# A decode-attention kernel: three value loads paired in the load order, output projection on two column groups, last selection over two PSUM banks

## The chip, the cores and the metric

One NeuronCore of a Trainium2 (trn2) chip. The metric is the device time of one execution in microseconds (us), the median of several executions on the slowest (here: only) core. The span of a profile is some 1.8 us shorter than the time. Ratios are computed from runs of the same rounds on the same chip: the mean time of one kernel's fast runs over the mean of the other's, so they are not quite the ratio of the medians quoted beside them.

## The reference

One decoding step for 32 sequences with 32 query heads and 8 key/value heads of 128, over the last 512 positions of the cache:

```python
B, Sq, D = x.shape                      # 32, 1, 512
Hq, Dh = 32, 128
W = min(4096, max(256, Sk // 4))        # 512
q = (x @ wq)                            # -> 32 heads of 128
k = repeat(k_cache[:, :, Sk - W:, :], 4, axis=1)
v = repeat(v_cache[:, :, Sk - W:, :], 4, axis=1)
p = softmax(einsum("bhqd,bhkd->bhqk", q, k) * Dh ** -0.5)
o = einsum("bhqk,bhkd->bhqd", p, v)
return o.reshape(B, Sq, Hq * Dh) @ wo   # bf16 throughout
```

Keys and values of the window are 33.6 MB each, wq and wo 4.2 MB each: 75.5 MB must be read for very little arithmetic.

## The kernel before

Sixteen key loads K0..K15 and sixteen value loads V0..V15 of 2 MB go through one DMA queue (the sync engine's) in a fixed order, into three key buffers and four value buffers. VectorE transposes each key load (T), TensorE makes scores (S), VectorE and ScalarE the softmax (M, E, R, N), TensorE turns P (P, then C), both engines spread it into a block form (Z), and TensorE multiplies it with the values (V). The orders are written out by hand for every engine.

```python
DMA_ORDER = ("K0 K1 K2 V0 K3 K4 V1 K5 K6 K7 V2 K8 K9 V3 K10 V4 K11 K12 V5 K13 K14 V6 K15 V7 V8 V9 V10 V11 V12 "
             "V13 V14 V15").split()
DVE_ORDER = ("T0.0 T0.1 T1.0 T1.1 T2.0 T2.1 M0 R0 T3.0 Z0.0 ...").split()   # cut; the query comes ahead of it
...
nc.sync.dma_start(w_sb[:, 0:2, :]..., wq_rows[:, 0:wq_half])      # first half of wq
@block.sync
def _(sp):
    sp.dma_start(w_sb[:, 2:4, :]..., wq_rows[:, wq_half:])        # second half
    for name in DMA_ORDER:
        n = int(name[1:])
        if name[0] == "K":
            if n >= NK: sp.wait_ge(dve_T, 2 * (n - NK + 1))       # NK = 3: transposed, buffer free
            sp.dma_start(K_sb[:, n % NK]..., cache_rows(k_cache, n)).then_inc(sem_k[n % NK], 16)
        else:
            if n >= NV: sp.wait_ge(pe_PV, n - NV + 1)             # NV = 4: multiplied, buffer free
            sp.dma_start(V_sb[:, n % NV]..., cache_rows(v_cache, n)).then_inc(sem_v[n % NV], 16)
    ...                                                           # then wo in nine pieces
```

The end, on TensorE, VectorE and ScalarE (the last two share the copies):

```python
select(SELCUT, B, lambda i: S_ps[:, 0, i * NHG * nl:(i + 1) * NHG * nl])   # the last 8 sequences, one bank
for hg in range(NHG):                                  # 8 pieces of wo
    pe.wait_ge(sem_wo[hg], 16)
    for i in range(4):
        if hg == NHG - 1 and i == WO_CUT: pe.wait_ge(sem_last, 16)
        for c in range(4):                             # four column groups of 32
            ins = pe.matmul(X_ps[32*c:32*(c+1), 2, 0:128], lhsT=o_sel[:, i, hg, :],
                            rhs=wo_sb[:, hg, i, c*128:(c+1)*128], ..., tile_position=(0, 32*c))
...
for c in range(2):                                     # VectorE; ScalarE takes c = 2, 3
    dve.tensor_copy(out_sb[:, c, :], X_ps[32*c:32*(c+1), 2, 0:128])
```

## Time and profile before

| | before |
|---|---|
| time, median of the first 3 runs | 187.69 us (187.65 to 187.70) |
| profiled span | 185.9 us |
| bytes moved by the load queue | 75.53 MB |
| last piece of wo: first, median, last of 16 DMA engines done | 179.78, 181.30, 182.99 us |
| store of the result issued | 183.98 us |

A load runs on 16 DMA engines; the trace records when each of them reports its share complete. "First, median, last engine" below are these completion events of one load, in us from the span's start. The page's rows, the waits and the tail are shown and read in the prediction.

### The profile page before, as it was taken

How to read it: one execution, taken by the hardware profiler on the slowest of the kernel's cores; microseconds unless marked ns; L12 is line 12 of the kernel's file. 1: busy time of each engine (PE TensorE's matmuls, PEld its weight loads, DVE VectorE, ACT ScalarE, POOL GpSimd, SP SyncE). 2: the span in 40 equal slices, each digit the busy share in tenths (PEclk: the TensorE clock that was granted, in tenths of full speed). 3: DMA queues.
4: the chain of work that ended last, by engine and by line, in shares of the span. 5: the costliest groups of instructions: out<-in, count | busy, mean ns of one | idle time of the engine just before them, and what ended most of it. 6: DMA issues, size and time to landing. Idle time of an engine off the chain costs nothing.

```text
span 185.9 us, 3842 instructions
## 1 busy us (share of the span) xinstructions
PE 109.0 (59%) x1604; PEld 89.4 (48%) x1604; DVE 131.9 (71%) x239; ACT 82.3 (44%) x142; POOL 32.0 (17%) x82
## 2 busy tenths in 40 slices
PE   0232004336179906929906994159979975998752
PEld 0100001022069805819606974019949975987741
DVE  0006999689999999993699987999999995010001
ACT  3001000269320397020695018925998999910011
POOL 7100390500700080060240041000040000000000
PEclk9999999955557985885985599576999999999998
DMA  6999999999999999999999999999999999999980
GB/s 194 434 448 412 437 423 423 448 412 437 420 416 441 416 427 434 416 437 427 423 421 423 441 423 420 434 423 430 428 412 434 427 423 430 420 423 411 405 332 27
DMA packets 6304, 75.80 MB, mean 408 GB/s; under 512 B 720, under 2 KB 912, under 8 KB 1936
## 3 DMA queue, kind: packets, MB, share of 16 engines
q1 hardware_dynamic: 6240, 75.53, 96.4%
q8 instruction: 12, 0.20, 0.4%
q10 hardware_dynamic: 48, 0.03, 0.1%
q14 instruction: 4, 0.03, 0.0%
HBM read 75.53 MB, written 0.03 MB: 406 GB/s over the span
## 4 chain that ended last, share of the span: by engine, by line
DMA 64%; DVE 20%; PE 9%; issue 3%; SPq 3%; DVEq 0%
DMA V_sb<-in_v_cache_dram 31%; DMA K_sb<-in_k_cache_dram 14%; DMA w_sb<-in_wo_dram 12%; DVE KT_sb L431 12%; PE O_ps L356 8%; DMA w_sb<-in_wq_dram 6%; DVE w_sb L453 4%; DVE QA_sb L421 2%; SPq L214 2%; PE X_ps L299 1%; SPq L202 1%; DVE oT_sb L414 0%; DVE KT_sb L409 0%; PE X_ps L393 0%; DVE maxv L438 0%
## 5 line engine op out<-in xcount | busy, mean ns | idle before, releaser
L431 DVE STREAM_TRANSPOSE KT_sb<-K_sb 128x2048 uint32<-128x2048 uint32 x32 | 72.3, 2287 | 1.3 <-DMA K_sb<-in_k_cache_dram 1.1
L356 PE MATMUL O_ps<-w_sb,V_sb 128*128 128x128 bf16 x640 | 47.0, 244 | 9.6 <-DVE w_sb L453 5.0
L356 PEld LDWEIGHTS O_ps<-w_sb,V_sb 128*128 128x128 bf16 x640 | 45.6, 110 | 12.3 <-DVE w_sb L453 6.5
L268 POOL COPY QBD<-QA_sb 32x64 bf16<-32x64 bf16 x64 | 25.6, 540 | 81.2 <-PE S_ps L319 63.6
L520 ACT ACTIVATE w_sb<-PTc,mask 128x512 bf16<-128x512 bf16 x60 | 38.9, 729 | 0.0
L319 PE MATMUL S_ps<-KT_sb,QBD 128*32 128x512 bf16 x256 | 20.7, 475 | 26.6 <-DVE KT_sb L431 20.2
L453 DVE TENSOR_SCALAR w_sb<-PTc,mask 128x512 bf16<-128x512 bf16 x100 | 30.2, 370 | 6.3 <-PE O_ps L356 6.3
L319 PEld LDWEIGHTS S_ps<-KT_sb,QBD 128*32 128x32 bf16 x256 | 7.5, 110 | 36.5 <-issue 32.4
L492 ACT ACTIVATE X_ps<-S_ps,negmax 128x512 f32<-128x512 f32 x8 | 5.3, 657 | 42.8 <-DVE negmax L440 42.8
L338 PE MATMUL PT_ps<-P_bf,pick 128*128 128x128 bf16 x128 | 11.4, 260 | 17.9 <-ACT P_bf L501 14.7
L338 PEld LDWEIGHTS PT_ps<-P_bf,pick 128*128 128x128 bf16 x128 | 9.8, 119 | 20.9 <-ACT P_bf L501 16.3
L530 ACT ACTIVATE oT_sb<-O_ps 128x128 bf16<-128x128 f32 x8 | 6.0, 750 | 28.2 <-PE O_ps L356 28.2
L356 PE MATMUL O_ps<-K_sb,V_sb 128*128 128x128 bf16 x256 | 14.9, 217 | 3.5 <-DMA V_sb<-in_v_cache_dram 2.2
L356 PEld LDWEIGHTS O_ps<-K_sb,V_sb 128*128 128x128 bf16 x256 | 14.5, 96 | 4.3 <-issue 2.5
L520 ACT ACTIVATE K_sb<-PTc,mask 128x512 bf16<-128x512 bf16 x24 | 15.3, 725 | 1.6 <-DVE KT_sb L431 1.6
L453 DVE TENSOR_SCALAR K_sb<-PTc,mask 128x512 bf16<-128x512 bf16 x40 | 12.1, 377 | 0.3 <-ACT PTc L511 0.2
L474 DVE CAST K_sb<-S_ps 128x256 bf16<-128x256 f32 x1 | 0.4, 425 | 14.3 <-PE S_ps L368 14.3
L356 PE MATMUL O_ps<-KT_sb,V_sb 128*128 128x128 bf16 x128 | 7.5, 217 | 2.3 <-DMA V_sb<-in_v_cache_dram 2.3
L356 PEld LDWEIGHTS O_ps<-KT_sb,V_sb 128*128 128x128 bf16 x128 | 7.3, 96 | 2.5 <-issue 2.5
L520 ACT ACTIVATE KT_sb<-PTc,mask 128x512 bf16<-128x512 bf16 x12 | 7.7, 728 | 0.0
L501 ACT ACTIVATE P_bf<-X_ps,recip 128x512 bf16<-128x512 f32 x8 | 5.5, 684 | 4.5 <-DVE recip L446 4.4
L409 DVE CAST KT_sb<-X_ps 128x512 bf16<-128x512 f32 x1 | 0.7, 692 | 9.2 <-PE X_ps L299 9.2
(41 smaller groups left out, 49.6 us busy)
## 6 DMA issues: line engine op xcount, KB each, us to landing
K_sb<-in_k_cache_dram SPq DMA_DIRECT2D x16, 2048.0 KB, 15.1
V_sb<-in_v_cache_dram SPq DMA_DIRECT2D x16, 2048.0 KB, 16.8
w_sb<-in_wq_dram SPq DMA_DIRECT2D x2, 2048.0 KB, 9.7
w_sb<-in_wo_dram SPq DMA_DIRECT2D x7, 512.0 KB, 19.8
w_sb<-in_wo_dram SPq DMA_DIRECT2D x1, 384.0 KB, 22.6
w_sb<-in_wo_dram SPq DMA_DIRECT2D x1, 128.0 KB, 14.4
oT_sb<-in_x_dram ACTq DMA_DIRECT2D x1, 32.0 KB, 4.4
out_dram<-oT_sb SPq DMA_DIRECT2D x1, 32.0 KB, 1.5
```

What stands on the lines that cost most here:

```text
L214: sp.dma_start(wo_sb[:, hg, i0:i1].rearrange("p i n -> p (i n)"), wo[hg * 512:(hg + 1) * 512, :].rearrange("(m i) n -> m (i n)", i=4)[:, i ...
L268: pool.tensor_copy(dst[:, i, :, x0:x0 + 4], src).then_inc(pool_qbd, 1)
L319: ins = pe.matmul(S_ps[32 * c:32 * c + 32, q % 2, :], lhsT=QBD[:, q % 2, g, b, e, :], rhs=bass.AP(tensor=KT_sb, offset=s0 * slot + (b * G ...
L338: ins = pe.matmul(PT_ps[:, r, :], lhsT=pick[:, r, KS - s:KS - s + P], rhs=P_bf[:, s, :], start=(s == 0), stop=(s == KS - 1), tile_position ...
L356: ins = pe.matmul(O_ps[:, q % 2, 0:P], lhsT=V_sb[:, m % NV, r, :], rhs=z_of(q)[:, :, x0 + r, :], start=(e == 0 and r == 0), stop=(e == 1 a ...
L421: dve.tensor_copy(QA[32 * a:32 * a + 32, c], QW[32 * c:32 * c + 32, :, :, a::4].rearrange("p h k q -> p h q k"),).then_inc(dve_q, 1)
L431: dve.transpose(KT_w[:, n % NK, b].rearrange("p i r s -> p r i s"), K_w[:, n % NK, :, 32 * b:32 * b + 32],).then_inc(dve_T, 1)
L453: ins = dve.tensor_scalar(z_of(q)[:, k].rearrange("p x r -> p (x r)"), PTc[:, q % RING].rearrange("p x r -> p (x r)"), mask[:, k:k + 1], N ...
L492: act.activation(P_f32, S_ps[:, q % 2, :], ACTF.Exp, bias=negmax[:, q:q + 1], scale=SCALE, accum_out=sums[:, q:q + 1],).then_inc(act_exp, 1)
L501: act.activation(P_bf[:, :, :], P_f32.rearrange("p (x s) -> p s x", s=KS), ACTF.Copy, scale=recip[:, q:q + 1],).then_inc(act_P, 1)
L520: ins = act.activation(z_of(q)[:, k].rearrange("p x r -> p (x r)"), PTc[:, q % RING].rearrange("p x r -> p (x r)"), ACTF.Copy, scale=mask[ ...
L530: act.activation(oT_sb[:, :, 4 * q:4 * q + 4].rearrange("p h a -> p a h"), O_ps[:, q % 2, 0:P].rearrange("p (a h) -> p a h", a=4), ACTF.Co ...
```

## The change

Its intent: fewer, larger value loads (V0+V1, V4+V5, V6+V7 are each one DMA of 4 MB into two neighbouring buffers); K0 ahead of the second half of wq, so that VectorE can transpose while it would otherwise wait for the query; engine orders matched to it; at the end the last O tile and half of the last selection moved so that VectorE and ScalarE work side by side on two banks; and two matmuls of 256 columns for four of 128, so that one copy per engine remains.

```diff
-        "K0 K1 K2 V0 K3 K4 V1 K5 K6 K7 V2 K8 K9 V3 K10 V4 K11 K12 V5 K13 K14 V6 K15 V7 V8 V9 V10 V11 V12 "
-        "V13 V14 V15"
+        "K0 B0 K1 K2 K3 V0 K4 K5 K6 V2 K7 K8 V3 K9 K10 K11 V4 K12 K13 K14 V6 K15 V8 V9 V10 V11 V12 V13 V14 "
+        "V15"
 ... PE_ORDER, DVE_ORDER ("T0.0 T0.1 Q0 T1.0 ...") and ACT_ORDER likewise ...
+    V_PAIRED = (0, 4, 6)
-                    if n >= NV:
-                        sp.wait_ge(pe_PV, n - NV + 1)
+                    k = 2 if n in V_PAIRED else 1
+                    if n + k > NV:
+                        sp.wait_ge(pe_PV, n - NV + k)
                     sp.dma_start(
-                        V_sb[:, n % NV]..., cache_rows(v_cache, n)
+                        V_sb[:, n % NV:n % NV + k]..., cache_rows(v_cache, n, k)
 ...
-            select(SELCUT, B, lambda i: S_ps[:, 0, i * NHG * nl:(i + 1) * NHG * nl])
+            select(SELCUT, B, lambda i: S_ps[:, i // 2, (i % 2) * NHG * nl:(i % 2 + 1) * NHG * nl])
-                    for c in range(4):
+                    for c in range(2):
-                            X_ps[32 * c:32 * (c + 1), 2, 0:128],
+                            X_ps[32 * c:32 * (c + 1), 2, 0:256],
 ...
-            for c in range(2):
-                dve.tensor_copy(out_sb[:, c, :], X_ps[32 * c:32 * (c + 1), 2, 0:128])
+            dve.tensor_copy(out_sb[:, 0, :], X_ps[0:32, 2, 0:256])
 ... ScalarE: one copy of 256 columns; half of the last selection copy; the last O copy goes to VectorE ...
```

## The prediction

> **What bounds the kernel now.** I read the overview page first, then the sync engine's waits, then the last 10 us of the timeline, then a table by stage.
>
> ```profile
> PE 109.0 (59%) x1604; PEld 89.4 (48%) x1604; DVE 131.9 (71%) x239; ACT 82.3 (44%) x142; POOL 32.0 (17%) x82
> ...
> DMA  6999999999999999999999999999999999999980
> GB/s 194 434 448 412 437 423 423 448 412 437 420 416 441 416 427 434 416 437 427 423 421 423 441 423 420 434 423 430 428 412 434 427 423 430 420 423 411 405 332 27
> ...
> q1 hardware_dynamic: 6240, 75.53, 96.4%
> q8 instruction: 12, 0.20, 0.4%
> ```
>
> No compute engine is over 71%, but the row DMA has a 9 in every slice from the second to the 38th, and the rate stays between 405 and 448 GB/s there. The loads are one unbroken stream of 75.5 MB.
>
> ```profile
> K_sb<-in_k_cache_dram SPq DMA_DIRECT2D x16, 2048.0 KB, 15.1
> V_sb<-in_v_cache_dram SPq DMA_DIRECT2D x16, 2048.0 KB, 16.8
> ```
> ```profile
> SPq L202 <- DVE KT_sb L431: 94.6, 13, 21.6
> SPq L208 <- PE O_ps L356: 40.7, 7, 17.9
> SPq L219 <- ACT oT_sb L547: 13.4, 1, 13.4
> ```
>
> The queue waits 94.6 us for transposes and 40.7 us for value products before it may issue. That looks like the bound, and the chain of waits counts 20% for VectorE accordingly. It isn't: from issue to landing a load takes 15 to 17 us (median, first fence), although 2 MB move in 4.9 us, so each is issued with about two others still ahead of it. The shortest issue to landing in the trace is 10.7 us (a key load), still 5.8 us of queued work. The loads' completion events land every 4.89 us (median engine: 13.04, 17.94, 22.84, 27.73, ...), without a gap at any wait.
>
> ```profile
> core 0: us, PE busy (x) PEld busy (x) DVE busy (x) ACT busy (x) POOL busy (x), PEclk, DMA share, GB/s
> ...
> 111.00:156.00 45.00, 33.71 (x528) 29.55 (x525) 42.85 (x113) 37.59 (x66) 3.28 (x6) 0.89 1.00 425
> 156.00:171.00 15.00, 11.61 (x196) 11.48 (x197) 0.69 (x2) 7.85 (x14) 0.00 (x0) 1.00 1.00 421
> 171.00:179.40 8.40, 5.93 (x144) 5.49 (x144) 0.42 (x1) 0.72 (x1) 0.00 (x0) 1.00 1.02 405
> 179.40:183.00 3.60, 1.73 (x91) 1.09 (x77) 0.00 (x0) 0.00 (x0) 0.00 (x0) 1.00 0.38 146
> ```
>
> Even at 111 to 156 us, where VectorE is busy 42.85 of 45 us, the DMA share is 1.00. After 179.4 us the share falls to 0.38: most DMA engines have finished and a few run late. The completion events show it: all 16 engines land a load within 0.38 us of each other up to 47 us, within 1.8 us after that, within 3.3 us at the end. Each step follows one of the twelve 16 KB packets of the instruction queue: such a packet (about 1.05 us, and the next data packet lasts 1.1 instead of 0.61) makes one engine about 1.6 us late for good. Three engines are hit twice, and they set the last landing at 183.0 us; the mean engine is done about 1.8 us earlier.
>
> ```profile
> 178.24 0.42 DVE L474 CAST K_sb<-S_ps 128x256 bf16<-128x256 f32 x1 [14.28 <-PE S_ps L368]
> 178.72 1.30 PE L393 MATMUL X_ps<-w_sb,K_sb 128*32 128x128 bf16 x80 [0.52 <-DVE K_sb L474]
> ...
> 182.71 0.56 PE L393 MATMUL X_ps<-w_sb,K_sb 128*32 128x128 bf16 x16 [0.55 <-DMA w_sb<-in_wo_dram]
> 183.32 0.56 ACT L547 ACTIVATE oT_sb<-X_ps 32x128 bf16<-32x128 f32 x2 [5.81 <-PE X_ps L393]
> 183.32 0.59 DVE L477 CAST oT_sb<-X_ps 32x128 bf16<-32x128 f32 x2 [4.66 <-PE X_ps L393]
> 183.98 0.36 SPq L220 DMA_DIRECT2D out_dram<-oT_sb  x1
> ```
>
> The selection (its second copy ends at 178.66) and the output projection have caught up with the stream by 180.0 and then wait for each piece of wo. On the path after the last landing lie only the last four matmuls (to 183.3), the copies (to 183.91) and the store (to 185.9).
>
> **What the Trainium skill says.** (1) "DMA: Bandwidth & Descriptors", Where 436 GB/s comes from: 16 ports of 256 bits at 850 MHz give 435.2 GB/s. The trace agrees: the second to 36th slices average 427. (2) The same page, Measured, advises transfers of at least 1 MiB, and its anatomy section fits about 2.0 us fixed per DMA, on the software path. Merging two loads would pay that only where loads run one by one; landings 4.89 us apart for 8 packets of 0.614 us per engine leave no such gap here. (3) "Runtime: NRT & Kernel Launch", Instruction fetch mechanics: refills come in 16 KiB blocks of 256 instructions, TensorE holds 128 KiB, and crossing a block is "mostly hidden". The trace agrees on the blocks (twelve packets of 16 KB for some 3250 TensorE records); hidden from TensorE they are, but not from a saturated DMA engine. (4) "PSUM — Partial Sum Buffer", PSUM bank collisions: two engines may not touch the same bank and partition quadrant at once. So letting VectorE and ScalarE share the second selection copy needs two banks; no run here shows a collision.
>
> **The change part by part.**
>
> *Three value pairs (0+1, 4+5, 6+7).* Bytes are the same. Three DMAs fewer means three fewer completion packets per engine, at 9 ns each: 0.03 us. A pair has 32 KB per partition contiguous on both sides, so its packets may become 32 KB. The trace's packets took 46 ns (1 KB), 160 (4 KB) and 614 (16 KB): 37.8 ns per KB plus 8.7. If the packets double, each engine saves 8 x 8.7 ns = 70 ns a pair, 0.21 us for three. Estimate: 0.03 to 0.24 us, on the path. A fetch's 1.6 us stays.
>
> *K0 ahead of the second half of wq.* K0 lands at 13.2 instead of 18.1, the half at 18.1 instead of 13.2. VectorE transposes K0 (2 x 2.23 us) at 13.2 to 17.7, when it was idle. The query then starts when the half has landed: 18.1 + 1.9 for its matmuls = 20.1, + 6.3 us for copy, transpose and 16 copies = 26.4 (before: 15.2 to 21.5). T1 ends at 30.9, T2 at 35.4; before, T2 ended at about 34.8. Nothing is won or lost downstream.
>
> *Does the stream stay fed?* A load must be issued before the load ahead of it lands. With landings at 8.3 + 4.9 per load, walking the new order with durations of the old trace: K4 needs T1 (30.9), its slot opens at 42.5. K6 needs T3, which follows the first scores (3.6 us at the low clock), the maximum and R0: about 41; slot 53. K7 needs T4, behind Z0 and M1: about 53.4; slot 63.7. K10 needs T7, behind the first two value products (4.6 us each, to 60.4), M2 and Z1: about 75.4; slot 83.2. K11 needs T8: 79.9; slot 88. V4+V5 needs two products (60.4); slot 93. K14 needs T11: about 105.6; slot 112.6. V6+V7 needs four products (86.4); slot 117.5. V10 needs product 6, whose data now lands with its partner at 127.3: about 131; slot 142. The least slack is about 7 us. No starvation, so the reordered VectorE, ScalarE and TensorE work is worth 0.
>
> *Selection and last evacuation.* VectorE copies the last O tile (about 0.3 to 0.7 us, where ScalarE took 0.72), and the two engines each copy half of the selection (128x128 instead of 128x256 in 0.42 us). The projection may start some 0.3 us earlier than 178.7. It then waits for wo until 183.0 anyway: 0 on the path.
>
> *Output projection.* 64 matmuls of 256 columns instead of 128 of 128. The last 16 took 0.41 us to the end of the last when nothing held them back, so (0.41 - 0.22)/15 = 13 ns apart with four column groups. Two groups of twice the width should come 53 ns apart (estimate: half the array), about 107 ns per block of wo against 51: 3.4 us in all instead of 1.7. There is room: the 28 blocks before the last wo piece need 3.0 us from 178.5. After the last landing, one matmul of 256 takes about 0.27 us (193 ns at 64 columns, 219 at 128, 245 at 192) and the second follows 53 ns later, so TensorE ends 0.04 to 0.08 us later than before. Then VectorE makes one copy of 256 columns, about 0.425 us (its 128x256 copy above) against 0.59 for two: -0.165. ScalarE's single copy is about 0.38 (0.27 at 128 columns, 0.49 at 384), so VectorE's ends last. Net: about -0.1 us.
>
> *Fewer TensorE instructions.* 128 fewer load and matmul records, all at the end, is half a block. The twelfth fetch (180.9 us) may come later or fall away; it hits an engine that is not among the three latest. The double hits come from the ninth to eleventh fetches, 151.8 to 172.0, which stay: 0.
>
> Sum: -0.1 for the tail and -0.03 to -0.24 for the pairs: -0.13 to -0.34. 187.69 - 0.25 = 187.4 us.
>
> **The rivals.** *A starved queue*: the pair takes two slots at once and delays K15 behind V6+V7. For: TensorE runs at half clock in places (PEclk 5 in mid-kernel), and my walk is coarse. Against: 7 us of slack. It would cost 1 to 5 us and show as slices under 400 GB/s. *Other fetch luck*: if the double hits vanish the end comes up to 1.6 us earlier (186.0); if one engine is hit three times before the end, 1.6 us later (189). For: the fetches follow TensorE's progress, which the new order shifts. Against: the ninth to eleventh fall well before the last loads in either order. *The tail as the bound*: the two-group projection falls behind the wo stream; by its 3.4 us against the time from 178.5 to 183.0 it has about 1 us to spare. Failing, it costs 0.2 to 0.5 us. *The compute chain is the bound*, as the chain's 20% for VectorE suggests, and the reorder wins 2 to 4 us (184 to 185.5). Against: DMA share 1.00 throughout; fewer bytes or a better rate alone could do that, and the port limit leaves 2%.
>
> **Range and chances.** The three runs of before agree within 0.05 us. The pairs and the tail span 0.2 us; fetch luck and a small stall make up the rest: 186.7 to 188.0. Faster by over 2% means below 183.9, under what this stream allows without losing all engine skew: 3%. Slower by over 2% needs a long starvation: 2%.
>
> **What would show it.** Right: the DMA row still full from the second slice, 75.5 MB, landings 4.89 us apart, last wo landing within 0.4 us of 183.0, one final copy per engine of about 0.43 and 0.38 us, final matmuls waiting for wo. Wrong: slices under 400 GB/s before 170 us, engine spread at the end far from 3.3 us, a projection that doesn't wait for wo, or a last landing moved by more than a microsecond.

## The result, and the profile after

The changed kernel takes 187.24 us (187.13 to 187.36, 6 runs) against 187.67 us (187.29 to 187.85, 6 runs): ratio 0.9981, 95% interval 0.9968 to 0.9994. So it is faster by 0.3 to 0.5 us, about a fifth of a per cent: clear of noise.

The overview page after: busy times, the DMA rows in 40 slices, the two queues, the chain of waits.

```profile
PE 109.5 (59%) x1540; PEld 90.3 (49%) x1540; DVE 132.1 (71%) x239; ACT 81.2 (44%) x141; POOL 31.8 (17%) x82
...
DMA  6999999989999999999999999989999999999980
GB/s 201 428 445 424 431 421 484 445 367 424 424 421 445 413 435 421 428 435 410 458 438 392 445 410 442 463 382 442 415 431 431 410 438 417 438 410 416 400 338 30
...
q1 hardware_dynamic: 5808, 75.53, 96.5%
q8 instruction: 12, 0.20, 0.4%
...
DMA 41%; PE 22%; DVE 20%; ACT 7%; issue 6%; SPq 3%
```

Bytes and busy times are as before, 64 matmuls are gone, and the load queue carries 432 packets fewer: 384 for the pairs (768 packets of 16 KB have become 384 of 32 KB in the records) and 48 completion packets. The slices with an 8, or with 367, 392 and 382 GB/s, look like holes but aren't: one or two slices ahead of each stand 484, 458 and 463, more than any slice of before. The low slices lie at the ends of the three pairs (which land at 42, 101 and 125 us), and the page books a long packet's bytes in one slice. The run unpaired_2 below, the same order without pairs, has no slice under 409 GB/s from the second to the 37th (172 us). Longer stretches have no such edges (columns: busy us and count of each engine, granted clock, DMA share, GB/s):

```profile
core 0: us, PE busy (x) PEld busy (x) DVE busy (x) ACT busy (x) POOL busy (x), PEclk, DMA share, GB/s
...
10.00:47.00 37.00, 10.42 (x100) 4.26 (x96) 29.69 (x46) 8.03 (x15) 11.87 (x31) 0.99 1.01 430
47.00:111.00 64.00, 38.68 (x519) 32.77 (x520) 54.98 (x75) 25.59 (x45) 10.78 (x28) 0.74 1.01 428
111.00:156.00 45.00, 36.34 (x538) 31.97 (x536) 40.98 (x101) 35.87 (x63) 4.73 (x10) 0.81 1.01 426
...
179.40:183.00 3.60, 2.97 (x50) 2.15 (x44) 0.00 (x0) 0.00 (x0) 0.00 (x0) 1.00 0.31 117
```

The stream is as full as before. Only the chain of waits tells another story: 64% DMA before, 41% after, with 22% for TensorE. Nothing about the bound has changed; the chain just entered compute at other places, because wherever the queue waits for a buffer the chain may follow the buffer instead of the stream.

The issues of the loads (number, KB, median us from issue to landing):

```profile
K_sb<-in_k_cache_dram SPq DMA_DIRECT2D x16, 2048.0 KB, 15.0
V_sb<-in_v_cache_dram SPq DMA_DIRECT2D x10, 2048.0 KB, 15.4
V_sb<-in_v_cache_dram SPq DMA_DIRECT2D x3, 4096.0 KB, 23.4
```

And the tail (start, duration, engine, what):

```profile
178.03 0.29 DVE L487 CAST K_sb<-S_ps 128x128 bf16<-128x128 f32 x1 [0.81 <-PE S_ps L375]
...
178.41 2.80 PE L400 MATMUL X_ps<-w_sb,K_sb 128*32 128x256 bf16 x48 [0.41 <-DVE K_sb L487]
...
182.45 0.61 PE L400 MATMUL X_ps<-w_sb,K_sb 128*32 128x256 bf16 x8 [0.33 <-DMA w_sb<-in_wo_dram]
183.10 0.38 ACT L563 ACTIVATE oT_sb<-X_ps 32x256 bf16<-32x256 f32 x1 [4.80 <-PE X_ps L400]
183.10 0.41 DVE L489 CAST oT_sb<-X_ps 32x256 bf16<-32x256 f32 x1 [4.78 <-PE X_ps L400]
183.57 0.36 SPq L223 DMA_DIRECT2D out_dram<-oT_sb  x1
```

The projection still waits for wo (0.33 us before its last piece but one; the last small piece is then taken without a visible wait, each two matmuls 0.11 us after the two before, so nothing is to spare there). The two final copies take 0.41 and 0.38 us where two rounds took 0.59 and 0.56. From the last landing to the store's issue it was 182.99 to 183.98, 0.99 us; now it is 182.72 to 183.57, 0.85 us. So the profiled span is 0.4 us shorter: 0.27 us in the stream and 0.14 us in the tail.

### The profile page after: what moved, and what is told of

Read it like the earlier page. It is cut to its first block, busy times and chain, and to the rows that moved or that the text cites. A ratio compares the mean times of both kernels' runs of the same rounds, so it can differ in the third digit from the quotient of the medians.

```text
span 185.5 us, 3711 instructions
## 1 busy us (share of the span) xinstructions
PE 109.5 (59%) x1540; PEld 90.3 (49%) x1540; DVE 132.1 (71%) x239; ACT 81.2 (44%) x141; POOL 31.8 (17%) x82
## 4 chain that ended last, share of the span: by engine, by line
DMA 41%; PE 22%; DVE 20%; ACT 7%; issue 6%; SPq 3%
PE O_ps L361 16%; DMA V_sb<-in_v_cache_dram 11%; DMA w_sb<-in_wo_dram 11%; DVE KT_sb L439 10%; DMA K_sb<-in_k_cache_dram 10%; DMA w_sb<-in_wq_dram 9%; DVE w_sb L461 5%; PE S_ps L322 4%; ACT w_sb L530 4%; DVE QA_sb L429 2%; SPq L217 2%; ACT KT_sb L530 1%; PE PT_ps L341 1%; DVE maxv L446 1%; PE X_ps L302 1%
## 5 line engine op out<-in xcount | busy, mean ns | idle before, releaser
L361 PE MATMUL O_ps<-w_sb,V_sb 128*128 128x128 bf16 x640 | 45.4, 240 | 10.0 <-DVE w_sb L461 5.1
L361 PEld LDWEIGHTS O_ps<-w_sb,V_sb 128*128 128x128 bf16 x640 | 44.2, 108 | 12.0 <-issue 6.1
L461 DVE TENSOR_SCALAR w_sb<-PTc,mask 128x512 bf16<-128x512 bf16 x100 | 31.1, 379 | 2.3 <-ACT PTc L521 1.1
L341 PE MATMUL PT_ps<-P_bf,pick 128*128 128x128 bf16 x128 | 12.6, 277 | 24.6 <-ACT P_bf L511 20.0
L341 PEld LDWEIGHTS PT_ps<-P_bf,pick 128*128 128x128 bf16 x128 | 10.9, 128 | 28.2 <-ACT P_bf L511 22.8
L540 ACT ACTIVATE oT_sb<-O_ps 128x128 bf16<-128x128 f32 x7 | 5.2, 742 | 16.9 <-PE O_ps L361 16.9
L461 DVE TENSOR_SCALAR K_sb<-PTc,mask 128x512 bf16<-128x512 bf16 x40 | 10.7, 346 | 2.4 <-ACT PTc L521 2.4
L302 PE MATMUL X_ps<-w_sb,oT_sb 128*32 128x512 bf16 x32 | 3.8, 627 | 10.6 <-DMA w_sb<-in_wq_dram 10.6
L482 DVE CAST oT_sb<-O_ps 128x128 bf16<-128x128 f32 x1 | 0.7, 711 | 12.9 <-PE O_ps L361 12.9
L496 ACT ACTIVATE KT_sb<-X_ps 128x512 bf16<-128x512 f32 x1 | 0.6, 597 | 17.3 <-PE X_ps L302 17.3
```

The lines of the kernel that those rows point to most:

```text
L302: ins = pe.matmul(X_ps[32 * c:32 * c + 32, k, :], lhsT=xT_sb[:, kt, :], rhs=w_sb[:, kt, c * 1024 + k * 512:c * 1024 + (k + 1) * 512], star ...
L341: ins = pe.matmul(PT_ps[:, r, :], lhsT=pick[:, r, KS - s:KS - s + P], rhs=P_bf[:, s, :], start=(s == 0), stop=(s == KS - 1), tile_position ...
L361: ins = pe.matmul(O_ps[:, q % 2, 0:P], lhsT=V_sb[:, m % NV, r, :], rhs=z_of(q)[:, :, x0 + r, :], start=(e == 0 and r == 0), stop=(e == 1 a ...
L461: ins = dve.tensor_scalar(z_of(q)[:, k].rearrange("p x r -> p (x r)"), PTc[:, q % RING].rearrange("p x r -> p (x r)"), mask[:, k:k + 1], N ...
L540: act.activation(oT_sb[:, :, 4 * q:4 * q + 4].rearrange("p h a -> p a h"), O_ps[:, q % 2, 0:P].rearrange("p (a h) -> p a h", a=4), ACTF.Co ...
```

## The experiments

The completion events of the last piece of wo, in the profiled execution of each kernel (us), beside the timing. "Packets" says whether the value pairs are 32 KB packets.

| kernel | packets | first | median | last engine | ratio to before (95% interval) |
|---|---|---|---|---|---|
| before | 16 KB | 179.78 | 181.30 | 182.99 | 1 |
| before_twocols | 16 KB | 179.69 | 181.22 | 183.24 | 0.9983 (0.9969 to 0.9997) |
| unpaired | 16 KB | 179.82 | 181.23 | 183.35 | 0.9982 (0.9965 to 0.9998) |
| unpaired_2 | 16 KB | 179.76 | 181.10 | 182.98 | 0.9987 (0.9974 to 0.9999) |
| the changed kernel | 32 KB | 179.38 | 180.92 | 182.72 | 0.9981 (0.9968 to 0.9994) |
| after_again (the same) | 32 KB | 179.42 | 181.01 | 182.70 | 0.9973 (0.9961 to 0.9985) |
| after_3 (the same) | 32 KB | 179.42 | 180.92 | 182.88 | 0.9982 (0.9969 to 0.9994) |
| fourcols | 32 KB | 179.48 | 180.96 | 182.68 | 0.9980 (0.9963 to 0.9996) |
| pe_pad | 32 KB | 179.44 | 181.00 | 182.84 | 0.9979 (0.9966 to 0.9993) |
| dve_repeat | 32 KB | 179.43 | 181.21 | 182.58 | 0.9975 (0.9963 to 0.9988) |
| wqfirst | 32 KB | 180.09 | 181.61 | 183.39 | 1.0020 (1.0003 to 1.0036) |
| pairs5 | 32 KB | 182.08 | 183.50 | 185.36 | 1.0039 (1.0008 to 1.0071) |
| wqfirst_v0 | 32 KB | 183.38 | 184.85 | 187.39 | 1.0147 (1.0128 to 1.0167) |
| wo_low8 | 32 KB | 180.63 | 183.20 | 184.69 | 1.0138 (1.0096 to 1.0180) |

unpaired, fourcols, wqfirst and before_twocols ran on one chip; the later runs, in two calls, on another (before has medians of 187.91 us on the first, 187.66 and 187.57 us on the second). For the first comparison (187.24 against 187.67 us) the record names no chip. Every output was correct.

### The pairs undone, twice

```diff
-    V_PAIRED = (0, 4, 6)
+    V_PAIRED = ()
-  ... K3 V0 K4 ... K11 V4 K12 ... V6 K15 V8 ...
+  ... K3 V0 V1 K4 ... K11 V4 V5 K12 ... V6 V7 K15 V8 ...
```

> The changed kernel with the three pairs loaded as six single loads in the same places (V0 V1, V4 V5, V6 V7); all else as changed. Packet theory (the stream is saturated, and each 32 KB packet saves a fixed cost over two of 16 KB): all data packets are 16 KB again, the slowest engine lands the last wo piece 0.2 to 0.4 us later than the changed kernel's 182.7, so about 183.0, and the time is 0.2 to 0.4 us over the changed kernel's: 0.05 to 0.15 us under before. Rival, the new order and the earlier K0 brought the gain: nothing lost, 0.35 to 0.45 under before. Rival, luck of the instruction fetches: the last landing moves by 0.3 or more in a direction that follows the number of twice-hit engines and not the packets.

Measured: 187.53 us (187.39 to 187.82), 0.38 us under before's median on that chip, about what the changed kernel had gained in the first comparison. The landings said the opposite: last engine at 183.35, median at 181.23. Because the two did not agree, it ran again in one call with the changed kernel.

> The changed kernel once more, so that it stands on one chip beside the variants of this call. From its first six runs: ratio to before 0.998, 0.2 to 0.5 us under before; last wo landing at 182.6 to 183.0.

> The changed kernel again, as the mark for this call: 0.997 to 0.9985 of before; last wo landing 182.6 to 183.0; three DMA engines over 3 us late at the end.

> The unpaired variant again, now on the same chip as the changed kernel, because its first timing (0.38 us under before, on another chip) did not agree with its landings (0.3 to 0.6 us later than the changed kernel's). Packet theory: median engine's last landing 0.25 to 0.35 us after the changed kernel's, and 0.2 to 0.4 us more time. Rival, pairing is worth nothing in time: equal within 0.1 us.

Measured: 187.35 us (187.24 to 187.60; the queue has 6240 packets again, as before) against 187.28 us (187.17 to 187.43) for the changed kernel; median engine 181.10 against 180.92, first engine 179.76 against 179.42. The time difference, 0.07 us, is below what five runs resolve, and below the 0.2 us that the packet theory asked for. The landings are clearer, above all those of the first engine, the one least delayed by instruction fetches: in the six profiles with pairs and an unbroken stream it ends at 179.38 to 179.48, in the four without at 179.69 to 179.82, a difference of the means of 0.33 us, with no overlap; the last engines (182.58 to 182.88 against 182.98 to 183.35) don't overlap either. Directly, a pair takes 9.71, 9.69 and 9.71 us from one landing to the next (first engine), where two loads take 2 x 4.89 = 9.78: 0.07 to 0.09 us each, about 0.24 us for three. The packets say the same: 1218 ns for 32 KB, 614 ns for 16 KB, so 10 ns saved on each of 24 packets per engine. The first engine is not the same one throughout: where a fetch holds it up, the next one takes its place and the step grows by up to 0.16 us. The mean of all sixteen engines does not have this fault. Over the four profiles without pairs it is 181.12 us, over the five with pairs and the same twelve fetches (all six but pe_pad) 180.87: 0.25 us, what three pairs of 0.08 us give. The fetches are no rival here: each of these nine profiles has twelve, and three engines about 3 us late or more at the end.

### The tail alone, in both directions

fourcols is the changed kernel with the old end; before_twocols is the kernel before with the new one.

```diff
-                    for c in range(2):                        # fourcols; before_twocols is the reverse
-                        ins = pe.matmul(X_ps[32*c:32*(c+1), 2, 0:256], ..., rhs=wo_sb[:, hg, i, c*256:(c+1)*256])
+                    for c in range(4):
+                        ins = pe.matmul(X_ps[32*c:32*(c+1), 2, 0:128], ..., rhs=wo_sb[:, hg, i, c*128:(c+1)*128])
 ... and two copies of 128 columns per engine for one of 256 ...
```

> The changed kernel with the output projection on four column groups and two copies per engine at the end, as before. Tail theory: from the last wo landing to the store's issue takes 1.0 us again instead of 0.85, so 0.10 to 0.15 us slower than the changed kernel; the projection's matmuls take 1.7 us in all instead of 3.4 and wait for wo more. Rival, the two-group projection falls behind the wo stream and costs something: four groups are faster than the changed kernel.

> The kernel before with only the output projection on two column groups and one final copy per engine. Tail theory: 0.10 to 0.15 us faster than before, from the end of the path alone; last landing unchanged at 183.0. Rival, the saved instructions (128 fewer TensorE records) spare a fetch that mattered: more than 0.3 us.

The tail of fourcols, then that of before_twocols:

```profile
183.01 0.56 ACT L567 ACTIVATE oT_sb<-X_ps 32x128 bf16<-32x128 f32 x2 [4.84 <-PE X_ps L400]
183.01 0.59 DVE L490 CAST oT_sb<-X_ps 32x128 bf16<-32x128 f32 x2 [4.83 <-PE X_ps L400]
183.66 0.36 SPq L223 DMA_DIRECT2D out_dram<-oT_sb  x1
```
```profile
183.62 0.41 DVE L476 CAST oT_sb<-X_ps 32x256 bf16<-32x256 f32 x1 [5.10 <-PE X_ps L393]
184.08 0.36 SPq L220 DMA_DIRECT2D out_dram<-oT_sb  x1
```

From the last landing to the store: 182.68 to 183.66 is 0.98 us with four groups, 183.24 to 184.08 is 0.84 us with two. With the two kernels of the comparison (0.99 and 0.85) the tail is worth 0.14 us in both directions, within the 0.10 to 0.15 expected. The times don't show it: fourcols has the ratio of the changed kernel (0.9980), and before_twocols, at 0.9983, gained 0.37 us by the medians where 0.10 to 0.15 were expected; its interval reaches from 0.06 to 0.58 us. That it gained through something else is not excluded by its time, but its trace shows nothing else: it has twelve fetches like before, and its last landing is even later than before's (183.24).

### K0 behind wq again

```diff
-  "K0 B0 K1 K2 K3 V0 K4 ..."          # B0 is the second half of wq
+  "B0 K0 K1 K2 K3 V0 K4 ..."
-  "T0.0 T0.1 Q0 T1.0 ..."             # VectorE; Q0 is the query
+  "Q0 T0.0 T0.1 T1.0 ..."
```

> The changed kernel with the second half of wq ahead of K0 again and the query ahead of the first transposes on VectorE. Theory: the stream is the same packets in another order and never runs dry, so within 0.1 us of the changed kernel, although the query is ready about 5 us earlier. Rival, VectorE's chain counts (20% of the chain of waits): a change of 0.5 us or more.

Measured: 188.16 us (187.94 to 188.84), 0.25 us over before and about 0.65 us over the other two variants of the changed kernel on the same chip. The expectation was wrong. The queue's issues in this run, and the stretch after them:

```profile
1.72 24.73 SPq L204 DMA_DIRECT2D K_sb<-in_k_cache_dram  x4
26.49 0.60 SPq L211 DMA_DIRECT2D V_sb<-in_v_cache_dram  x1
```
```profile
25.00:30.00 5.00, 0.00 (x0) 0.00 (x0) 5.00 (x3) 0.00 (x0) 2.67 (x8) 1.00 0.97 364
```

The same stretch of the changed kernel:

```profile
25.00:30.00 5.00, 0.00 (x0) 0.00 (x0) 4.84 (x7) 0.00 (x0) 3.27 (x10) 1.00 0.99 419
```

(The columns are those of the stages shown before.) The changed kernel reads 419 GB/s in these five microseconds, this one 364. Four key loads are issued from 1.72 to 26.45; the fourth, K3, needs T0 finished, which without the early K0 happens at 25.9 us, so it went out at 25.91. The load ahead of it began to land at 27.45 and K3 landed at 33.08, 5.64 us later instead of 4.90: a hole of 0.74 us. In the old order V0, which needs no buffer to come free, stood in that place. The early K0 is therefore not a gain of its own but a condition of the new load order: K3 could then be issued at 17.71.

### The pair ahead of K3

```diff
-  "B0 K0 K1 K2 K3 V0 K4 ..."          # wqfirst
+  "B0 K0 K1 K2 V0 K3 K4 ..."          # V0 is the 4 MB pair
```

> The variant that loads the second half of wq first and turns the query first lost 0.73 us between the landings at 27.45 and 33.08, because K3 was issued at 25.9 (after T0) and stands ahead of everything else in the queue. Here the pair V0+V1 goes ahead of K3, as V0 did before; wq first and the query first stay. Theory, the queue ran dry only because K3 was next: no gap over 4.95 us between 16-packet landings, the last landing within 0.15 us of the changed kernel's, the time within 0.2 us of it. Rival, the earlier K0 is worth something by itself through VectorE's chain: still 0.4 us or more over the changed kernel.

Measured: 190.51 us (190.00 to 192.00), ratio 1.0147: far worse than what it was to mend. The profile is of the longest of these runs, so its losses are above those of the median run. The first hole is gone, but K3 now lands at 42.0 to 42.5 instead of 32.4 to 32.7, VectorE stands still for 7.0 us until then, and the transposes after it are late:

```profile
42.49 2.31 DVE L439 STREAM_TRANSPOSE KT_sb<-K_sb 128x2048 uint32<-128x2048 uint32 x1 [6.99 <-DMA K_sb<-in_k_cache_dram]
```

K7 is issued at 59.95 instead of 54.64. From 60 to 95 us this run, then the changed kernel:

```profile
60.00:95.00 35.00, 23.16 (x337) 20.17 (x339) 31.90 (x43) 15.49 (x28) 6.52 (x16) 0.82 0.98 380
```
```profile
60.00:95.00 35.00, 19.11 (x286) 14.93 (x283) 32.51 (x52) 20.38 (x36) 9.67 (x24) 0.84 1.02 432
```

380 GB/s, with a DMA share of only 0.98 against 1.02. Landing to landing it took 5.42, 5.20, (4.89,) 5.92, 6.18, 5.55 and 9.94 us where 4.89, or 9.70 for a pair, is the pace: 4.0 us in all, as much as its first engine is later at the end (183.38 against 179.38). (The last of these, at a pair issued 7.7 us ahead, is the first engine held up, not the queue: the other engines keep their spacing.) The theory that only K3's place mattered fell. VectorE's chain is not the bound, but it is only a few microseconds from being it.

### More pairs

```diff
-    V_PAIRED = (0, 4, 6)
+    V_PAIRED = (0, 4, 6, 8, 10)
```

> The changed kernel with V8+V9 and V10+V11 paired as well: five pairs. Packet theory: 128 x 2 more packets of 32 KB, each pair about 0.08 us shorter than two loads (9.71 us against 9.79 from landing to landing), so landings after V11 about 0.16 us earlier than the changed kernel's and the time 0.1 to 0.2 us under it, if the pairs are issued in time (V10+V11 needs product 7, at about 139, and its slot opens at about 141.7; V12 then needs product 8, whose data land at about 142). Rival, a pair that waits for two buffers lets the queue run dry: a landing gap over 10 us and a time up to 1 us longer.

Measured: 188.31 us (187.30 to 189.90), ratio 1.0039; the profile is of the longest of these runs, in which more is lost (first engine at 182.08, 2.7 us late) than in the median run (1.1 us over the changed kernel). The rival was right. The pair V10+V11 went out at 138.72, 1.07 us before the load ahead of it landed, and landed 10.88 us after it; V12 and V13 followed at 5.62 and 5.73 us, being issued 2.2 us ahead. This run's stretch, then that of the changed kernel:

```profile
147.00:157.00 10.00, 10.00 (x170) 8.78 (x168) 6.18 (x23) 5.49 (x11) 0.00 (x0) 0.96 0.91 341
```
```profile
147.00:157.00 10.00, 9.53 (x170) 9.36 (x167) 6.89 (x27) 10.00 (x19) 0.00 (x0) 1.00 0.99 419
```

Over all profiles, each load issued 2.7 us or less ahead of the landing in front of it left a hole of 0.3 us or more, and those issued 3.77 to 3.94 us ahead (one load in each of four profiles) left none: they landed 4.88 to 4.98 us after the load in front. Between 2.7 and 3.77 us there is no case. The changed kernel's two tightest are 4.15 us (V10) and 4.86 us (K10); in its two other profiles V10 had 5.10 and 3.77 us, K10 4.41 us in both.

### Useless work on VectorE

```diff
+                    if q == 1:                                # ahead of the second spread
+                        for k in range(3):
+                            dve.tensor_reduce(spare[:, k:k + 1], PTc[:, 1]..., AX.X, ALU.max)
```

> The changed kernel with three useless reductions of 512 columns (about 0.6 us each, 1.8 in all) on VectorE ahead of the first part of the second spread, near 61 us. The tightest key load after it (K10) was issued 4.86 us before the load ahead of it began to land, and gaps showed in other runs where this lead was under about 2.7 us; 1.8 us less leaves about 3. Theory: no landing gap over 5.1 us, the time within 0.2 us of the changed kernel. Rival, VectorE's chain is the bound: 1.5 to 1.8 us longer.

```profile
61.09 1.88 DVE L463 TENSOR_REDUCE spare<-PTc 128x1 f32<-128x512 bf16 x3
```

Measured: 187.18 us (187.03 to 187.29), ratio 0.9975: nothing lost. No landing took over 4.93 us. Part of the 1.88 us went into time in which VectorE would have waited: K10 still had a lead of 4.23 us, little under the 4.41 to 4.86 us of the three profiles without the extra work. So this much work on VectorE, at this place, is free because the leads last, and the chain of waits, which gives VectorE 20%, overstates it.

### Two more instruction fetches

```diff
+            def pad(n):
+                for _ in range(n):
+                    pe.matmul(O_ps[0:32, 1, 0:32], lhsT=ident, rhs=ident, start=True, stop=True, ...)
+            pad(40); ... pad(110); ... pad(106)               # in TensorE's idle time up to 31 us
```

> The changed kernel with 256 useless small matmuls (512 more TensorE records, two blocks of 256) in TensorE's idle time up to 31 us. Theory, each refill of 256 instructions makes one DMA engine 1.6 us late for good, in turn over eight engines: two more instruction packets, 14 in all, every one from the second on about two places earlier; at the end five engines instead of three are over 3 us late and none is hit three times, so the last landing stays within 0.2 us and the time within 0.3 us, while the median and the mean landing come later (the mean by 2 x 1.6 / 16 = 0.2 us). Rival, fetches fall on engines at random: the number of late engines does not rise by two, or one engine is 4.5 us late or more.

```profile
q8 instruction: 14, 0.23, 0.5%
```

Measured: 187.28 us (187.11 to 187.45), equal to the changed kernel. Fourteen fetches, and at the last piece of wo five engines are 2.92, 2.98, 3.17, 3.21 and 3.40 us behind the first, where the changed kernel has three (3.39, 3.43, 3.47) and the next is at 2.01. The last fetch comes too late to matter in both (180.6 us here), so 13 fetches count instead of 11. 8 + 5 and 8 + 3 are what a rotation over eight engines gives, and random placing would hardly have given it together with no engine over 3.5 us. The mean of the sixteen came 0.10 us later (180.97 against 180.87), half of the 0.2 us expected.

### One piece of wo on eight engines

```diff
+                    if hg == 3:
+                        for p0 in range(0, P, 8):
+                            sp.dma_start(wo_sb[p0:p0 + 8, hg, :]..., wo[...][p0:p0 + 8, :]).then_inc(sem_wo[hg], 16)
```

> The changed kernel with one 512 KB piece of wo (the fourth) loaded as sixteen DMAs of 8 partitions, each of which should run on 8 of the 16 DMA engines (eight of the sixteen increments should come at once, the other eight with the data). The eight engines used get 64 KB instead of 32, the others none: about 1.2 us more for the first and less for the second. Theory: instruction fetches go in turn to eight of the sixteen engines, those that are 1.5 us or more late at the end, and the last landing is theirs. If the eight used are the unhit ones, their landings of this piece come within 0.8 us of each other and the last landing of all comes up to 1.2 us earlier, the time 0.5 to 1.2 us under the changed kernel; if they are the hit ones, 1.2 us later, and the time 1.2 over; a mixture shows lateness of both kinds. Rival, the lateness does not belong to fixed engines: no change over 0.3 us.

```profile
w_sb<-in_wo_dram SPq DMA_DIRECT2D x16, 32.0 KB
```

Measured: 190.06 us (189.13 to 191.65), ratio 1.0138. Eight increments of each small DMA did come at once, so eight engines were used. But all engines ended later, the first too (180.63 against 179.4), and the 4 KB packets took 201 ns on average instead of 163, so the shifted work can't be told from the cost of the small DMAs. Whether the twice-hit engines are among the eight used stays open, and with it whether a lopsided last load could win back part of the 1.9 us between the mean and the last engine (180.81 and 182.72 in the changed kernel).

None of the variants beats the changed kernel beyond noise.

## Why the prediction was right

**The bound.** It said that the stream of 75.5 MB sets the time, so that reordered compute is worth nothing. The DMA share stayed 1.01 over 10 to 156 us, and unpaired, which has all of the new order, lands its last load where the old order does (182.98 and 183.35 against 182.99 and 183.24). Shown.

**The pairs, 0.03 to 0.24 us.** The packets became 32 KB, the branch that gave 0.21 to 0.24. Direct measure: 0.07 to 0.09 us per pair, about 0.24 us together; the mean landing of the sixteen engines says 0.25 us. The upper end of the range. In time it is not resolved (0.07 us, five runs each).

**The tail, about 0.1 us.** Copies 0.41 us (predicted 0.425) for 0.59; TensorE 0.05 us later after the last landing (0.38 against 0.33; predicted 0.04 to 0.08). Sum 0.14 us, seen in four kernels. The two-group projection keeps up, though with less to spare at the last piece than the "about 1 us" of the prediction.

**Selection on two banks, 0 on the path.** The projection starts at 178.41 us instead of 178.72, the 0.3 us earlier that was expected, and waits for wo after it as before.

**Instruction fetches.** Twelve as before (the twelfth again at 180.8 us, too late to matter), three engines twice hit, last landing moved by under 0.3 us. The rotation over eight engines, only suggested by the record of before, passed the test of two more fetches. One detail was read too simply: not each step in the engines' spread follows one of the twelve. Four packets of 8 KB of another instruction queue (q14, at 52.1, 53.3, 88.7 and 134.2 us) come with smaller steps, under 1 us each. That fits a ninth late engine, beside the eight of the rotation. The spread in mid-kernel is up to 2.1 us, not 1.8.

**Stream fed, least slack about 7 us.** The conclusion held; of the working a part did. Against the last engine's landing of the load in front, as the prediction counted, the least slack was 6.1 us (V10) and 6.7 us (K10). Most issue times were met: K4 30.87 us (30.9 expected), K7 54.64 (53.4), K10 76.38 (75.4), K11 80.77 (79.9). Three things were wrong. V10 went out at 135.65 instead of 131: product 6 did not start when its data landed (127.04) but when VectorE's spread was done (129.1), and it took 6.4 us where 3.7 had been left for it (127.3 to 131). The slot was read from the last engine, but the first one runs dry first, and its landing is 1.8 us (K10) to 1.95 us (V10) earlier; the 5.8 us of queued work under "issue to landing" is too high for the same reason (3.88 us at the first engine). And any lead over zero was taken as enough, where holes appear from about 2.7 us down. Counted so, the tightest load of each of the three profiles (4.15, 4.41 and 3.77 us) was only 1.1 to 1.7 us above the leads that left holes. That the order survived with so little is in part luck. By the same rule wqfirst (K3 1.53 us ahead) would have been safe.

**K0 ahead of wq: "Nothing is won or lost downstream".** True of the whole change, wrong as an account of the part: without it the new load order loses 0.74 us at K3.

**A bad test of its own.** The prediction named slices under 400 GB/s before 170 us as a sign that it was wrong. Three such slices appeared, where pairs end, and none in the same order without pairs: they come of 32 KB packets booked in one slice. A full stream has to be judged by longer stretches and by the spacing of the landings.

The predicted gain of about 0.25 us (0.13 to 0.34) stands against 0.43 us by the medians and 0.36 us (0.19% of 187.67) by the ratio.

## What to carry to other kernels

When the DMA row is full from end to end, ask of each change only what it does to the bytes, to the fixed cost of the packets, to the lead of each load and to what follows the last landing; the chain of waits can shift its shares by twenty points without any of these moving. Keep a lead table (landing in front minus issue) for every load: here a load had to be issued about three microseconds ahead, and a load order is only right together with the compute order that frees its buffers in time. Small gains are read more surely from the landings of the DMA engines (the first repeats within 0.1 us here, the mean of the sixteen within 0.2) than from five timings that scatter by 0.3 us.

## What the Trainium skill lacked or had wrong

- "Runtime: NRT & Kernel Launch", Instruction fetch mechanics, calls the cost of a block boundary mostly hidden. For a saturated stream it lacks the price: each 16 KB fetch (about 1.05 us) leaves one DMA engine about 1.6 us late for good, in a rotation that fits eight engines (the ninth fetch is the first to hit an engine twice; eleven that came before the end gave three twice-hit engines, thirteen gave five). At the end the last engine is 1.9 us behind the mean.
- "DMA: Bandwidth & Descriptors", Measured, counsels transfers of at least 1 MiB, and its table of single transfers goes on to 16 MB, but it has no figure for merging loads that are queued one behind another. Here two queued 2 MB loads made into one of 4 MB saved 0.07 to 0.09 us, by packets of 32 KB in 1218 ns for two of 614 ns.
- The same page has no figure for how far ahead a load must be issued to keep the engines busy. Leads of 2.7 us and less left holes of 0.3 to 1.3 us; leads of 3.77 us and more left none.
- The same page, Where 436 GB/s comes from, says that for HBM to SBUF transfers the HBM side (about 358 GB/s) binds. The trace has 426 to 430 GB/s over stretches of 37 to 64 us, nearer to the port figure of the same section. Its note under Measured gives about 358 GB/s for the case that both cores of the HBM domain stream; the sentence itself lacks that condition.
- The same page, How many engines (k), is borne out: loads of 8 partitions used eight engines, eight increments coming at once. It lacks that sixteen such loads of 32 KB at the end of a saturated stream cost 2.9 us against the changed kernel of the same call (190.06 against 187.20).
